# State read and four-expert causal attention on one core: new orders for the five instruction queues

## Chip, cores, metric

One core of one Trainium2 chip. The metric is device time in microseconds (us), the median of repeated runs of one launch; lower is better.

## What is computed

`x` is (8 batches, 8 heads, 512 tokens, 64) and `state` (8, 8, 32, 64). A first attention reads in both directions; its result, 544 rows of 512 for each batch, is the input of a mixture of four causal attention experts, of which every row uses two.

```python
a = softmax(x @ state.T / 8); xread = a @ state        # 512 rows per head
a2 = softmax(state @ x.T / 8); sread = a2 @ x          # 32 rows per head
y = concat([xread, sread])                             # (8, 544, 512)
logits = y @ w_gate; w = softmax over the two largest logits
for e in range(4):
    q, k, v = y @ wq[e], y @ wk[e], y @ wv[e]
    out += w[e] * (softmax(causal(q @ k.T / 8)) @ v @ wo[e])
```

## The kernel before, in words

Most factors are kept as a pair of fp16 numbers, a high part and the rest, and a product of two such pairs is three matmuls (`PROD`, line 293). An op that makes a pair is `split`, `low` or `hi_lo` (lines 338 to 365): one instruction writes the high part, another the difference.

The work on a batch is in four groups.

- `front(b)` (line 556) splits and turns x, makes the scores against the state and their softmax (tiles `eb`, `sbm`, `et`), turns them (`at`), folds the weights into the state (`gs`), and from these makes values `v`, gate logits `lg`, keys `kt` and queries `qm`. `gate` (line 879) is a chain of short instructions over tiles `cmp`, `gt`, `gs`, `wgt`: differences, comparisons, sums, an exponential on ACT, a division.
- The main group: `probs` (line 919) makes scores of a block of 128 rows in PSUM, adds the mask and takes the row maximum on DVE (`masked`, the custom operation in the profile, out `p`), shifts (`mx`), exponentiates on ACT, splits into `ph` and transposes by DMA into `pt`. `reads` (line 963) multiplies by `v`, scales by the gate (`su`, `c`, `z`), splits (`zh`, or `zhp` for two blocks at once), transposes by DMA, and `result` (line 1021) multiplies by `wo` and writes out (`o`).
- `side(b)` (line 846) makes the state's own reads (`a`, DMA to `a2t`, PE into `xt_tail`).
- `tail(g)` (line 1063) does the attention of the 32 state rows of two batches at once (tiles that begin with t).

Nothing in this code fixes the order of the work. Each function records steps (class `Steps`, line 142); a step has an engine, one or more calls and the steps that it must follow. 1883 steps are recorded, and `run` (line 255) then issues them by three packed lists, `ORDER` (line 22): the order of all steps, for each step which of its alternative ways is used, and for each buffer which slot of its tile it gets. A way is another engine for the same operation (`either`, line 208, offers for instance ACT, POOL or DVE for a copy, and DVE or POOL for a difference) or, for a group of matmuls, the reverse order of its two halves. Each engine runs its own steps in the order of the list: 290 steps on PE, 654 on DVE, 527 on ACT, 238 on POOL, 174 DMAs on the SP queue. A step waits for its inputs and for the readers of the buffer that had its slot before.

```python
        for n in memoryview(steps).cast("H"):
            s = self.all[n]
            for f, kw in s["ways"][ways[n]][2]:
                f(**{k: v.ap() if isinstance(v, View) else v for k, v in kw.items()})
```

`takes_port` (line 191) marks steps for the planner that made the lists, and issues nothing: every POOL step, DVE differences and products with both inputs in SBUF, and DVE copies from SBUF to SBUF. Those steps are called port steps below. As all instructions come from line 265 of the loop above, the profile tells them apart by tile names.

Of the kernel before, what the change touches and what calls it, by code (L numbers as in the profile page):

```python
# [24 lines left out]
        "Uq}Y&AUCFlT;K;Gm>ddVN>~jQARB~27FY?ZAQjYt+E53|LmoU06`>LohD=ZjJs<(p1%=9R7D_-yC=F2%4aFe_3Swz2gkjhissKP$H~{tF3@}uK"
        "a}W%%kQWMLVrT;Ap*~!IOHdseKvSpzp;!}&U_-bJA&?)kLoqxAhoLAof_88buE15e2G=1E1VVZ^0>$wLbcPbx0k%U|2*)0f7nRCFN9YMHp*{41"
        "a?l&PKt3#q-Czy0g4VDXx<ednfj*EQ-_k)C05_p8?0^8+3H_iy41~ql3<g0bSc*%qIShs&5Q(>-7=*(zYyr1nISz#txDj?i1g^x2I2y)485{=t"
        "VIK?!qp9FQBVZ(qg2_+{rbAKK26tc&l!R3{1u9`>bQFcrxEklfZnz6$VFBEO888iI!a|q@YcK}KK{8qd;~^m}h7%BriK#4B!8WiJ=E4N1ik>tZ"
        "+QJf;16g4nOoT?b7L(9Ym;~$4mm1@8SOx{*5qQxGSdZ1P2|k7Q@ED%JGuRC8s3~rOlaPo$Ky~~G-c%ct(sO8r51=`|hL`XH%Hb=hgKr=V-a-rf"
        "0daT=KEY?Gk6)lXeuWy?05@PwybljyBPOSx@CzDZ1>A(c;RkKOcvKhT({HMUopBx4!ydR9x8f&ihd$H=dtp~>iGQFy_QVAAhg#uh8i3ufFQ%Zc"  # L30
        "G!Q%BAp8s6@f*B@Id~MN<5cX8-=QD&$H6!RhvG17jsKtzrljFG0!QK~oQxf@4W^<gNH_!M;xwFx{sfqoQd3);iJfp3GS0{G=tm1MK2E>{n1;I2"
        "XiP^l<O>O=r-bN<ir*-J#$aYxh$+#q8+E6Nn1>SKSe%68Fare=VqTh!Ug(WJ*n_^4!=DsHi!eLoqKuS}wqb5cg}>-M?ZoZ419zbZ9)k~*gZ@%#"
        "48oq2pW@+e+=qK{5AMeU=!Y3Gm_AY_I*i95k}^{oEI>Kw2xg&wbPyxqC?>{ZxR$e0T0Dc<s29~IU}fVVIDx^~n~;yA<5)V0(Nu=ka12G!Sv-V&"
        "C<zh^GZ&<!m<dZ$W(=jWw1H1y13HHuT#+krW$sJsIh;;o77U}p6pypwMlMI^F@z$h3UA_u)SUb=K3~MESe*J%A<Bl^cn|O73z!ZYQDZ7eRk;Ku"
        ";39MvxAQ%GgL`=wU&AJJAJgMzzK(HJk;;=VKEUjF32)#4s>V0*EpFjTREnzeJG_N6r2<u^DpZvA@k4x%33(t@r4Lw)a$q$|j)SN=)u5KNl|Nz)"
        "Zbz3fCl02XREug;Gpa*PsRgy74&=$Zxjpr#)|8an&<^fM$+#{(!g@565^+twg2Tv{lk+G1j9#3A1F#kkry(?gQgR)x%_FH3rNG-bibm67@#e=^"
        "m-n*|x1|I8jyuzPKFG&71CF7@e3Zx0SbBm<I2F$oKfZ%y;1D0-!<<%*^LYA#^W+CEkTm?6Pw;%2KojXFPNK=Qh`!<n?m`Rc7cP^NoSJ`Qab8UR"
        "vVi{J5^AJtC>cJ*61<hB&?!F6CHV{o;#yikOKCYRqjj{N((+0Q;Ds`kmdi)pNEvw>ZKn<7&%ykO&+;ZJ!b@Z`?VxnBi_*({$-=8>8hyhIoR!mY"
        "4lV$>`6cG$Je-UFVo}b^`8X5*!}Oe=Gjo81@lGns1-Kv=;$oaZ0y%<LNDLR|5Dw*1yqZe$bUMdN1?Ux?=L<Yb%5gXc$_#pjGbxg1ODxZ#*)&Jy"
        "&?0H9WjKzrad}1x;*}D`7x_8vru7meSNIssrFpcEuJa|n%B$o!t(G;iR<iRRBHAGP=^7uPjB=AN^E!#<%<^8o;~hRhw>Sbi=ndW|C+RL%;Cg(J"  # L40
        "HpyN(L<yvo-sTU|fa`M>X~?Ij5r35C`iwuxX=3t_2D*h>^Jn?OhpC0O*2dg~6Ut`slxF;#w@5sRFJJiuH|6Ghh91%pI!bM|qqgCf{E8n@TYgN{"
        "tOY-zVEH2V_$;;4tCUF|@mBdN5BNSmrN`Wk-|#c)!fo^gc2aLSN7tw&U#D;Kn!oW+{?5PnH$UO_+EQ;&d;Y=O<PSgOr~H?nQwRRX-S{ST<W>xV"
        "LXudviwTQJO1VYJC98PJ4oM^_q$}U1opOm%iH|f<mDG|=l1L|Za)+AgcM*EaIV7ia=UsA{lFASHCCxOu_{mTCEx9C*bmo1MTMo-^>8uUxnB<jw"
        "a-NP$F6_YvC7JZ(zT8z0$qU*q`K2EpkpA37hjKybr9Jg7_2NC^D;KDMbkif!LmS%^p32>|w-%BCJdE#Aj11@FdQ|SyKu#ljr8if#$1;uk=yX1z"
        "u~JSNYFUYs!V)SWQba~@QMn*9cqCVs2GUmt@l1XxeYl~`;@LckYe-F5z~!Zu)wSBzP%29!sUVHzq+XOK(odU8C8=(&<c-vl{(4I5*<fyB6{U&{"
        ";f1`2U(0B2A_MfPEaox%R%+O5d?r_<s$7*~a*-O@bE#=Bq_)(tCHzi`%OxoxC8d;HmOpZZ&Isx?IVWf3pMd@q($c~@LQlwO6&<LmVe*p3vgvg>"
        "t!K2FyrQNSF7@ra4AL=rQk>S2Q&Lx6({1t4I}#yxCB7!m8#0l{@nDUVA$n8l$t3pFTari<>OJWw&Fr+?mqj{M<7rD7spHv8JIMp-EDxovHMcn&"
        "s7radHj^M-#>2FWyrCA>(lTm&S<YQ$E<ciB&7_$%ize4mI*(UqEAiHq+QwQ-N<FIs#7A3MDjlndwY5#q)Vjt}sGl~MHZoDy+BjXR10}64*0xec"
        "2FZ9`q7Nvmp3^kyujw?K4%c<oLMG`vouZR<uq4rT*51<Vd|tupZN5&`1$tg5^9D<*m-K?}(+)O7mT7j)sZp{}12nhh(j$6Mr|B%+X!|vTCex1Q"
        "tDWqSZnAcgNAu}XovwLxwhonH(q1}9e%-By^?)AJ&bCU&$VKg9U2Ts};LWyL%V;+lE8V4s%+VP-PWI|$ov9zSkbc$i@<l)C1c}lD`dPneNiD1^"  # L50
        "d7?~`$r7zSrJ#P-ANo^&X(?T+AsVXdG)C9xDlV$)^|!`q5&ic+(P(5~V#PFCw%8Q;qY3S=4zMdaS4*p>g=t^uX5DRr7S|H$ZQE_IZ8c{ew#|0f"
        "M)k5Bx=GbGYa;6>X2YewjF8oQRR`J-^RaN<qC0h~Zqw}=<aTIpOKO4E!+P2-y{^5atj4oGHpsHL8=A~+>NSmTi7kowT98%MzLwl>YgU)dRnrKK"
        ")LYum?r1r^tG(==X0!y>->U0<O<~zxu=SQ)?tw0|8k*f|YG%viGFfi-P&2yamc!+7QzeJxv|5_e<#qX7epg!;TNcY@S?!TN)+ahm;&h3vu-ul?"
        "QrS{lV5zN-)X@UY&kDLUR=|Q?K`Ue{Ev*%{5c9W@lG%k?5zAwFZMtN$B5su}w5K{s^4V%zWIJuQ?XsfwOb^)}D`v&*h@G|)Hr7hoVJokdG@Xr>"
        "0GHqP+CF=(`|W@owPSYN3c14WyoI=fcGg1O8LOZttg=?ob5_cVx(u$E3v@A7QA^teyJE#%33t*;x>D|jz0lGw%-ykD7Hehgrj@hXcG)i3MGJRV"
        "?XF$32p8$fxH!9S4{f}Cu(}#%6D-ONwNv)MqFszDZ=dY5#kzW0!S2}?8*U%1tQ%%uZKO@K(Kf~=+aw!dQ|ysFws8Ay*X@UmvX?r}BJ7oZv!C|M"
        "Uh5lut5a>7O}7~~(`H#k`)#vrj?J}s_SBx)b1UcSYZ<F#aqgYYw-@$apICYK(jqOrRd5wuC0E&1wpaGoURxFSL94oWF2MfSKLhuFR~)-HR?Ss+"
        "Q5N4Na0#6_Pp8gYBIo6jx*E>gRj~|~%tc#G_ttz}a+kuTbUx0xRL;Y_v-g(RrFQ-<iA(4FTzZ$rrFH)S)?}nA"
    ),
    (  # L60
        "c-obfiw=b#3`05n|Bt?jqI6?$k(j8w)^07dW{vz4IzBW#D^+Z~n{Tr<Adq{ZKUc5fsxqRQPrRQO9O3=$0QNm6r*!~?7_o82KhE&D<AaWR43Ow`"
        "P8cnGx1P+vYJ)`HqeJXdeo8UPxok6*iPBOg+M@#)g&gFFI10F!C>DcTy+Q=a1YaeSR6M3~%lPSx0L#3xt5f6x&Se$}Eescf$;`z3-rj9Ng&0@X"
# [3 lines left out]
        "c-m!?2W|sF3<K5m{~w2=bqWyMNNx*7iq!4QW@ejZTAJBf>oM%#$D_^7)4a#3$8)v3o%Zn3cU$mD2krHzMy&-n{Sj1%NC7QEM54E=M5zdugmC_="
        "ZWc%8W3eLEZcjqWp1vF!wLcQ)fTDqDR4|5(Qei6!Scqp$OBDeY<vf?b_p=VmDz|OjV^1a1=}>~|SS07La{%C4H7!g9eIDuv3VJ+I2b{2Uq~W7H"
        "?_Xm1E}fFn*PyQ8sP0}Y%49;m?Vu!z=K~f*x}!A2pb{d|PII1!+mmzt$U|F|tjkvfsNnLM^)&2{nooyHErxK;XeA~)d?62JhD!?WIbrxaI7M@u"
        "ykZL7Qho;BP%~u6nJL+fLio!~>IdH#sK&8)Qz@#Kv!=z*YEMWmY2m&*#1MGKah7X}vF;51lbEm2i>{!~Gcg-OU;k|vL(~oY&~3uV(D{w3JoL}@"
        "vBN>i%udsYl-w}gt210FBQ+ZIgA0I{YDM&VYgp0l>S;Cj3Owt&v-e89SK)i`?B+JU0A-K{b^"  # L70
# [1153 lines left out]
```

## Time and profile before

| what | value |
|---|---|
| median of 3 runs (least to most) | 282.70 us (282.16 to 283.89) |
| the profiled execution's own time | 282.6 us |
| span of the profile, first to last instruction | 280.8 us |
| granted TensorE clock, mean over the span | 1.000 |
| busy: PE, DVE, ACT, POOL | 266.9, 253.0, 227.3, 180.6 us |
| chain that ended last, by engine | PE 58%, DVE 16%, ACT 10%, DMA 7%, POOL 5% |

A timeline row gives start and duration in us, engine, line, operation, the tile written and the tiles read, shapes, how many instructions were merged, and in brackets how long the engine stood idle before and what ended that. A group row gives the count, the busy time in us, the mean in ns, and the idle time before. A row of the chain gives start, length and what was on the path.

### The profile page before, as it was taken

How to read it: one execution, taken by the hardware profiler on the slowest of the kernel's cores; microseconds unless marked ns; L12 is line 12 of the kernel's file. 1: busy time of each engine (PE TensorE's matmuls, PEld its weight loads, DVE VectorE, ACT ScalarE, POOL GpSimd, SP SyncE). 2: the span in 40 equal slices, each digit the busy share in tenths (PEclk: the TensorE clock that was granted, in tenths of full speed). 3: DMA queues.
4: the chain of work that ended last, by engine and by line, in shares of the span. 5: the costliest groups of instructions: out<-in, count | busy, mean ns of one | idle time of the engine just before them, and what ended most of it. 6: DMA issues, size and time to landing. Idle time of an engine off the chain costs nothing.

```text
span 280.8 us, 9174 instructions
## 1 busy us (share of the span) xinstructions
PE 266.9 (95%) x3441; PEld 177.4 (63%) x3441; DVE 253.0 (90%) x748; ACT 227.3 (81%) x627; POOL 180.6 (64%) x251
## 2 busy tenths in 40 slices
...
GB/s 199 241 153 150 166 172 190 237 191 153 157 200 191 188 168 248 172 197 171 207 235 260 131 239 161 167 173 118 205 236 154 154 245 193 225 219 189 213 226 157
DMA packets 163853, 53.70 MB, mean 191 GB/s; under 512 B 142688, under 2 KB 159328, under 8 KB 163808
## 3 DMA queue, kind: packets, MB, share of 16 engines
...
## 4 chain that ended last, share of the span: by engine, by line
PE 58%; DVE 16%; ACT 10%; DMA 7%; POOL 5%; issue 3%; SPq 0%; DVEq 0%; POOLq 0%; ACTq 0%
PE bank L265 58%; DMA a2t<-a 4%; DVE xh L265 2%; DMA pt<-ph 2%; ACT p L265 2%; DVE eb L265 1%; DVE sbm L265 1%; DMA xn<-in_x_dram 1%; POOL ph L265 1%; POOL eb L265 1%; DVE a L265 1%; ACT v L265 1%; DVE et L265 1%; ACT kt L265 1%; POOL at L265 1%
## 5 line engine op out<-in xcount | busy, mean ns | idle before, releaser
L265 ACT ACTIVATE p<-p,mx 128x256 f32<-128x256 f32 (+3 forms) x88 | 45.9, 557 | 3.1 <-POOL mx L265 2.3
L265 PE MATMUL bank<-gs,at 128*128 128x260 f16 (+3 forms) x296 | 40.7, 285 | 1.7 <-DVE z L265 1.6
L265 PE MATMUL bank<-v,pt 128*128 128x65 f16 (+1 forms) x660 | 40.8, 218 | 0.9 <-DMA pt<-ph 0.5
L265 PE MATMUL bank<-kt,qm 64*128 64x128 f16 (+7 forms) x384 | 40.5, 298 | 0.8 <-DVE z L265 0.6
L265 PEld LDWEIGHTS <-pt 128*128 128x128 f16 x660 | 37.7, 98 | 5.7 <-issue 2.3
L265 POOL TENSOR_TENSOR ph<-p,ph 128x1024 f16<-128x1024 f32 (+1 forms) x19 | 38.4, 2021 | 3.8 <-ACT tlg L265 1.3
L265 DVE CUSTOM_DVE_ANT_0 p<-bank,band 128x384 f32<-128x384 f32 (+3 forms) x88 | 39.4, 480 | 1.0 <-PE bank L265 0.6
L265 PE MATMUL bank<-at,gs 128*128 128x512 f16 (+1 forms) x128 | 32.7, 393 | 0.5 <-DVE v L265 0.5
L265 PEld LDWEIGHTS <-qm 64*128 64x128 f16 (+1 forms) x384 | 19.8, 95 | 18.0 <-issue 8.0
L265 PEld LDWEIGHTS <-at 128*128 128x128 f16 x264 | 25.1, 97 | 9.2 <-issue 2.1
L265 PE MATMUL bank<-wo_n,z 128*128 128x512 f16 (+1 forms) x114 | 26.1, 368 | 1.1 <-DMA z<-zh 0.5
L265 DVE SCALAR_TENSOR_TENSOR xh<-xn,xh 128x512 f16<-128x512 f32 x28 | 21.3, 778 | 1.5 <-ACT xh L265 0.9
L265 PE MATMUL bank<-wo_n,zp 128*128 128x512 f16 x84 | 20.1, 380 | 0.0
L265 ACT ACTIVATE ph<-p 128x1024 f16<-128x1024 f32 (+1 forms) x20 | 19.7, 983 | 0.2
L265 PEld LDWEIGHTS <-gs 128*128 128x128 f16 x120 | 11.4, 98 | 12.2 <-issue 1.2
L265 ACT ACTIVATE o<-bank 128x512 f32<-128x512 f32 (+1 forms) x30 | 16.9, 575 | 1.8 <-PE bank L265 1.2
L265 PEld LDWEIGHTS <-z 128*128 128x128 f16 x114 | 10.6, 98 | 12.0 <-issue 1.9
L265 POOL TENSOR_TENSOR at<-et,at 128x512 f16<-128x512 f32 x10 | 12.7, 1274 | 6.0 <-DVE cmp L265 4.2
L265 PEld LDWEIGHTS <-xh 128*128 128x128 f16 x416 | 14.1, 98 | 3.9 <-DVE xh L265 1.4
L265 ACT ACTIVATE v<-bank 128x256 f16<-128x256 f32 x40 | 15.4, 403 | 1.3 <-PE bank L265 0.8
L265 ACT ACTIVATE gs<-bank 128x260 f16<-128x260 f32 (+3 forms) x33 | 15.7, 491 | 0.6 <-PE bank L265 0.5
L265 ACT ACTIVATE z<-bank,c 128x64 f32<-128x64 f32 x62 | 13.9, 331 | 2.6 <-POOL c L265 1.6
...
## 6 DMA issues: line engine op xcount, KB each, us to landing
...
pt<-ph SPq DMA_TRANSPOSE x30, 4.1
...
```

The source lines that it names most:

```text
L265: f(**{k: v.ap() if isinstance(v, View) else v for k, v in kw.items()})
```

## The change

Only the three packed lists differ; configuration, steps and calls are the same. Cut to its form:

```diff
@@ -21,53 +21,53 @@
 ORDER = (
     (
-        "c-jru1A7o^7y!`M-@@7!mR75^wQO#=p`n&-+qP}nwr$(CZM%Da#d(f5!~=r(V1OXt18E>3tOb9_3ArH&6ag<t3l4HXK1c)^pb)Hs^{@dvAt|H)"
...
+        "c-jTQ17HwP6ac{IzZO=l<ytkgS}j|PtF^7Rw3cn#wr$(CZQHhO+$9D8hIo(z3_PGPB!PSo9~9C-0$2;a-~|r+AQ7a8gpdr%LLiiaVvrI_f;VJ?"
...
```

Unpacked and set against the old lists (a step counts when the step before it on its engine is another one): 33 of 290 steps on PE follow another, 141 on DVE, 109 on ACT, 84 on POOL, 43 on the SP queue. Of the ways, 50 differ: 23 steps come to DVE and 16 leave it, 15 come to ACT and 18 leave it, 9 come to POOL and 13 leave it, and three groups of matmuls have their halves reversed. Of 962 buffers, 576 get another slot, 300 of them PSUM banks. From 98 to 180 us and after 228 us the order on PE is the old one. The differences that the prediction speaks of (step number, what it does, its start in the profile before):

```
start, 0 to 60 us
  eleven of the twelve warm-up matmuls (line 514) PE: changed places among themselves
  109, 380, 370  single matmuls, 36.31, 54.35, 54.46
                                                  PE: up to eight places earlier
  13   copy of the state tile sn, 6.32            ACT -> DVE, second there
  118  copy of v out of a bank, 22.48             ACT -> DVE
  122  copy of lg out of a bank, 23.65            ACT -> DVE
60 to 98 us
  766  DMA xT<-xh, 67.40                          SP: six places earlier
  768  maximum m<-bank, 774 turn eb<-bank, 72.12 and 73.36
                                                  DVE: from ahead of 636 to behind it
  636  difference a (then DMA a2t, PE step 638)   DVE: as above
  571, 589  PE values and a small product, 77.97  PE: from ahead of 638 to behind step 478 (83.69)
  616  PE product, 80.57                          PE: to behind 278 (86.20)
  643  PE xt_tail,wn, 89.20                       PE: from ahead of 618 (92.37) to ahead of 493 (84.69)
  593  sum gt<-cmp, 495 reciprocal su, 88.42 and 88.34
                                                  DVE: 593 now ahead of 495; 597 still next
  597  gt<-gt,gt, 88.74                           DVE, same neighbourhood
  475, 468  z sum and ph difference, 88.26, 88.70 POOL, still one behind the other
  578  v difference, 87.35, and 949, 955          DVE: 578 to behind 497 (91.75); 949 ahead, 955 behind
180 to 228 us
  1484 DMA a2t<-a, 176.22                         SP: four places earlier
  934  z sum, 187.96; 1486 a difference (two instructions), 193.38; 924 zh difference, 166.75
                                                  POOL: all three directly behind 1485 (180.33)
  925  DMA z<-zh, 186.11                          SP: ahead of 1289 (184.36)
  1226 copy of lg, 182.21                         ACT -> DVE
  1241 cmp, 184.66                                DVE: three places earlier
  1294 masked p, 185.73                           DVE: from ahead of 1247 to behind it
  1247 gt<-gt,gt, 186.42                          DVE, still behind 1292
  1130 PE v,pt, 188.46                            PE: from ahead of 1316 (188.97) to behind 926 (190.34)
  1128 ph difference, 195.21                      DVE -> POOL
  1709 sum s, 196.30                              ACT -> DVE, directly behind 1304 (195.00)
  1711 a, 199.63; 1330 mx, 206.45; 1144 zhp, 209.77
                                                  POOL -> ACT
  1715 a difference (two instructions), 206.23    DVE -> POOL
  1352, 1345  PE v,pt, 211.08 and 214.14          PE: each one or two places later
  1158, 1159, 1160 z and zh, 207.10, 207.64, 222.57
                                                  POOL: ahead of 1301 (202.84)
```

## Rows read from the trace of the kernel before

**Rows 1.** Busy time by engine in four stretches: us, then each engine, clock, DMA.

```profile
25.00:60.00 35.00, 34.32 (x514) 23.57 (x499) 33.53 (x91) 33.37 (x91) 24.34 (x37) 1.00 0.90 189
60.00:98.00 38.00, 34.65 (x481) 24.00 (x480) 36.34 (x99) 32.55 (x99) 27.02 (x33) 1.00 1.02 179
98.00:180.00 82.00, 81.99 (x1005) 54.96 (x1003) 78.68 (x236) 69.89 (x202) 60.81 (x72) 1.00 1.05 195
180.00:228.00 48.00, 45.62 (x653) 28.88 (x652) 45.19 (x144) 41.31 (x112) 35.48 (x41) 1.00 0.87 179
```

**Rows 2.** Chain that ended last, 21 to 36 us: start, us, what.

```profile
22.58 0.28 ACT v L265
...
24.77 10.00 PE bank L265 x221
```

**Rows 3.** Timeline, 88 to 93.3 us: start, us, engine, line, operation, tiles.

```profile
88.26 0.48 POOL L265 TENSOR_TENSOR z<-z 128x128 f32<-128x128 f32 x1 [3.42 <-ACT su L265]
...
88.42 0.22 DVE L265 TENSOR_REDUCE gt<-cmp 128x20 f32<-128x80 f32 x1
88.70 2.13 POOL L265 TENSOR_TENSOR ph<-p,ph 128x1024 f16<-128x1024 f32 x1
88.74 2.13 DVE L265 SCALAR_TENSOR_TENSOR gt<-gt,gt 128x20 f32<-128x20 f32 x1
...
92.37 1.16 PE L265 MATMUL bank<-gs,at 128*128 128x256 f16 x9 [1.60 <-DVE z L265]
```

**Rows 4.** Tile gt: one group of its instructions, ns least/median/most.

```profile
L265 DVE SCALAR_TENSOR_TENSOR gt<-gt,gt x9: 115/171/2129, 27.0 to 264.3; 128x16 f32<-128x16 f32 x5, 128x20 f32<-128x20 f32 x3, 128x4 f32<-128x4 f32 x1
```

**Rows 5.** Timeline of DVE, 184 to 189 us.

```profile
186.42 1.61 DVE L265 SCALAR_TENSOR_TENSOR gt<-gt,gt 128x16 f32<-128x16 f32 x1
```

**Rows 6.** Timeline of PE, 186 to 194 us.

```profile
190.34 1.47 PE L265 MATMUL bank<-wo_n,z 128*128 128x512 f16 x6 [0.48 <-DMA z<-zh]
192.38 0.83 PE L265 MATMUL bank<-kt,qm 64*128 64x384 f16 x12 [0.57 <-DVE z L265]
```

**Rows 7.** Timeline of POOL, 167.5 to 171 us.

```profile
167.82 0.69 POOL L265 TENSOR_SCALAR a<-e,s 128x512 f16<-128x512 f32 x1
168.47 1.05 POOL L265 TENSOR_SCALAR xn<-xn 128x512 f32<-128x512 f32 x1
```

**Rows 8.** Timeline of DVE, 167.5 to 171 us.

```profile
168.06 0.98 DVE L265 SCALAR_TENSOR_TENSOR xh<-xn,xh 128x512 f16<-128x512 f32 x1
```

**Rows 9.** Chain that ended last, 198 to 232 us.

```profile
222.63 4.93 DMA pt<-ph
...
227.61 4.61 PE bank L265 x51
```

**Rows 10.** Chain that ended last, 66 to 82 us.

```profile
72.21 0.60 DVE m L265
72.81 1.22 DVE eb L265 x2
...
74.96 4.16 DMA a2t<-a
```

**Rows 11.** Timeline of PE, 92 to 100 us.

```profile
97.67 1.46 PE L265 MATMUL bank<-wo_n,z 128*128 128x512 f16 x6 [0.39 <-DVE gs L265]
```

**Rows 12.** Timeline of POOL, 178 to 193 us.

```profile
180.33 0.69 POOL L265 TENSOR_SCALAR a<-e,s 128x512 f16<-128x512 f32 x1 [2.08 <-DMA a2t<-a]
185.23 1.16 POOL L265 TENSOR_TENSOR at<-et,at 128x512 f16<-128x512 f32 x1 [4.21 <-DVE cmp L265]
186.35 1.64 POOL L265 TENSOR_TENSOR ph<-p,ph 128x768 f16<-128x768 f32 x1
```

**Rows 13.** Timeline of POOL, 199 to 228 us.

```profile
199.63 0.69 POOL L265 TENSOR_SCALAR a<-e,s 128x512 f16<-128x512 f32 x1 [1.91 <-DMA a2t<-a]
...
206.45 0.57 POOL L265 TENSOR_SCALAR mx<-mx 128x2 f32<-128x2 f32 x1
...
209.77 1.26 POOL L265 TENSOR_SCALAR zhp<-z 128x256 f16<-128x256 f32 x1
```

**Rows 14.** Groups by line and form, POOL: count, busy us, mean ns, idle before.

```profile
L265 POOL TENSOR_TENSOR ph<-p,ph 128x1024 f16<-128x1024 f32 x11 | 24.6, 2238 | 1.5 <-ACT tlg L265 1.3
```

**Rows 15.** Groups by line and form, DVE.

```profile
L265 DVE TENSOR_TENSOR ph<-p,ph 128x1024 f16<-128x1024 f32 x9 | 11.2, 1242 | 0.5 <-ACT ph L265 0.3 <-POOL ph L265 0.2
L265 DVE SCALAR_TENSOR_TENSOR a<-e,s,a 128x512 f16<-128x512 f32 x14 | 10.7, 762 | 1.5 <-POOL a L265 1.2 <-ACT a L265 0.2
```

More of the change, by code (lines that the diff above doesn't have):

```diff
@@ L23 @@
     (
-        "c-jru1A7o^7y!`M-@@7!mR75^wQO#=p`n&-+qP}nwr$(CZM%Da#d(f5!~=r(V1OXt18E>3tOb9_3ArH&6ag<t3l4HXK1c)^pb)Hs^{@dvAt|H)"
[L25 to L58, printed above, removed]
-    ),
@@ L60 @@
-    (
-        "c-obfiw=b#3`05n|Bt?jqI6?$k(j8w)^07dW{vz4IzBW#D^+Z~n{Tr<Adq{ZKUc5fsxqRQPrRQO9O3=$0QNm6r*!~?7_o82KhE&D<AaWR43Ow`"
-        "P8cnGx1P+vYJ)`HqeJXdeo8UPxok6*iPBOg+M@#)g&gFFI10F!C>DcTy+Q=a1YaeSR6M3~%lPSx0L#3xt5f6x&Se$}Eescf$;`z3-rj9Ng&0@X"
-        "#_$~v6*;@QN`xw-stl*X?#$LIQ}f!96pc^bS{trnRTVPWg8z9WpRdnRjOqXKAba>GQ%>lz6PMdfe&eV*PBj*5AMD$;H!dc^0rmrh5CJ&"
-    ),
-    (
[L66 to L70, printed above, removed]
+        "c-jTQ17HwP6ac{IzZO=l<ytkgS}j|PtF^7Rw3cn#wr$(CZQHhO+$9D8hIo(z3_PGPB!PSo9~9C-0$2;a-~|r+AQ7a8gpdr%LLiiaVvrI_f;VJ?"
@@ new lines @@
+        "To?k$p&;ah;*bV1KyJ(mVNe=MKyL5{A6N(LVFP4@w2%q{paMigYAB2;pcWK@%8(yd!YWt|wc#{`Lkv^_f&%CX2z5Z96xM~aP!Ov^X)J@)pgL59"
+        "%uo-`Kpv<8=b%0ufLJ&W5zrW#LQN=yLC^$>;00&^m*654#fESh4nrJVfva#0isKO|h9&S2G=g?;9Xi7e=m6WHEVhSG>;Xxk7v#Z`*cG~fQeNx`"
+        "Eg=|oz)r{oMPUs@LKJj@T~G;nLo4V8MIaM|!dvPNTOc3ygx#<h4?-Up0DYk!^oN146q~^k90Y@52;77)Yz=#%95#nrFcjLrGW4JpFdA;dax}UF"
+        "D=-Gj<9^r(ZDANx!F@0lhQkOL38P>#ti<WC4OZb4sDSff4~zjvCtwClgPBkj??O1P#s#njXTd!f3*%rRjE9OCfz_}&`p_bX#JP}w64GLr0P|or"
+        "OoXH~3GzZCTmoxx4io@yT8GK$9j(X4SOb^BGVr2JkchUza(Dzy@F_foC-4kbz<X$hC*c9a;&a#x$*49q#n<o>KEOI|jvMeJB&HYe3Zk$Kyn(k+"
@@ new lines @@
+        "2T#Ed_ynJ!K7N4|bRSw^5~_p`p(a+wckmM$U>t75Ul5NPVqN?SKPVb&;TGJ4p7fhKV-M_t^{^do#;q8i{?Kpeg<bI*e4;<l65C@>{7kLzD-FQD"
+        "*a441Z|sKOVIU5|l=K(6V{7b)b8tHL!>QN?`{Q67f<y5iWQSqc2MLE`DjI<!aWam=DL5AaQ_~EbhVyWSq@lJr6Md-@GNz|lI3LGjTJpqnlz{}}"
+        "V@4W{iVH9SPQY)J3cHeFH=2ll=?mp1#7r~>6JmFojgv4D`cW3>K?`v#jzcfZPX6?h@=yRJ#+>w>Qe$4qMGieMkhbAY+>Sf&80^CLlm<Ug2<4-A"
+        "m;`s@K3s%paWC${{dfQaFc9-oX8K4$bQq6A4ho|qn1y~(I?PH(@gMah<p>I<UUU#MV^TbW$M6KE$82;QPhxLEHV&uy1YDlHaSb~r7CwZ`$uJ1d"
+        "VgV{mS+D`ca39*hW$6^2!z$d6Dv}3R<@H>F3Q;`Hihb!kmZNGMj2qb(xA7jniX~_#U%*D>$z`Z8oyKcekT&sMypG#>Gw<blcmo?#Hr&D&u^(l?"
@@ new lines @@
+        "wOpOEV@WDPO(>G?V<=t1{1Bgu(ja<+QB;WrPz+V32Uvsm@lD*tx3CKJr&xZA(NvX+(K}3z)#yDY;DPiIt5XfSj2|!sHm6b)OEoD3>(WQefrF_f"
+        "ZRI$sMYX98HKV3fkA_k^Do!ov5hmmgG*jBs5b8*+s5K?yMC`*UxF#p($JmCvIF5I7M%=-}C=;gSPxu*Y@o-ATbvQA1qPo1FM^J4ZNuwwU`{8YT"
+        "#|L;c9po`|jF0j-8cRv}IH%?-I9J-zc>00!<O`<dL;Ri>%MqSW>G&shrZoHu5A#P}AdBb;eqe82Na^JcPN2m!k;=m)noM6YCHl$&I>BA&H!hPu"
+        "c#=zSBR$1SXbo+pZy3rY*#}SaQ#`{fXelkHW%QY+&{|5*>nIbir-ibTe0d{fkc<+@%VisFr%zmz&+-OZBAIy;?VzmekGp6yO{HnHiu^d3LpTHH"
+        ";vAftbMkz7iGQ&e=i$5@#Q!iO=i@A#Ny_j}isbxUfD3YQ_7i_D$19{F7vjQPgiG;iD$UdB94{51S9qQ;@GObqvg|K2=o!wWFrF<DJd0-29GOFl"
```

31 lines of the change are left out of this document (added).

## The prediction, made before the changed kernel ran

> **What bounds the kernel now.** I read the busy times by stretch first [rows 1]. From 98 to 180 us PE has 81.99 us of work in 82.00, so nothing that happens on other engines there can show. It stands idle for 35.00 − 34.32 = 0.68 us between 25 and 60, for 38.00 − 34.65 = 3.35 between 60 and 98, and for 48.00 − 45.62 = 2.38 between 180 and 228. The new lists leave PE its work, so apart from the start these 6.4 us are the ceiling of any gain. In both idle stretches DVE is the busiest of the others (36.34 of 38.00, 45.19 of 48.00): it sets when PE can go on. At the start the chain of waits goes through copies on ACT, one of them a `v` of 0.28, until PE takes over at 24.77 for 10.00 us [rows 2].
>
> Then I looked for what ends PE's idle time. The longest is 1.60 us before the product at 92.37, ended by DVE's `z`. Up the DVE queue from there stands one instruction on 20 columns that took 2.13 us, from 88.74 to 90.87 [rows 3]. Its group has a median of 171 ns [rows 4], so 1.96 us of it were a wait inside the instruction. POOL had begun a subtraction 0.04 us earlier, at 88.70, and ended it at 90.83 [rows 3]. The same happens at 186.42: 1.61 us, 1.44 of them lost [rows 5]; PE then idles 0.48 at 190.34 and 0.57 at 192.38 [rows 6]. A DVE step with two inputs in SBUF that comes just after a POOL step stands until that ends.
>
> Who goes first when DVE already waits? POOL ran `a` from 167.82 to 168.51, the next POOL instruction is shown from 168.47 with 1.05 us [rows 7]; DVE's difference `xh` came at 168.06 and ended at 169.04 [rows 8]. DVE waited for the first and went ahead of the second. So the loser of a collision is whoever arrives after the other's start, and a waiting DVE step passes one POOL step, not two.
>
> Last, PE's 50 us of unbroken work to the end start at 227.61, behind a DMA `pt` of 4.93 us that POOL released at 222.6 [rows 9]. A gain made before that must also reach POOL there.
>
> **The change, part by part.** Sums are against the profiled execution, 282.6 us (span 280.8 and 1.8 around it); the median of the runs is 282.7.
>
> *Start.* Steps 118 and 122 leave ACT, and with 118 the 0.28 that stood on the chain [rows 2]: −0.3. The state copy 13 moves too, but PE's next step then waits for the input DMA anyway; nothing. The warm-up matmuls and the single matmuls 109, 380 and 370 change places beside waits of other engines; nothing. Bounds: −0.68, PE's whole idle time up to 60 [rows 1], and +0.3, if the copies come as late on DVE.
>
> *60 to 98 us, ahead of 638.* DVE made 768 (0.60) and 774 (half of 1.22) before 636, and 636 releases the DMA `a2t` of 4.16 us for which PE stands at 79.16 [rows 10]. With both behind it the DMA starts up to 1.21 earlier, or somewhat less, since 636 also needs ACT's high part. But 571 and 589, about 1.1 us of PE work, no longer fill that wait: PE loses up to 0.5 there. They are not lost: with 616 and 643 they now stand behind 638, where PE later waited. DMA 766 is earlier, but what follows it on PE waits for an ACT copy: nothing.
>
> *The step 597.* The sum 593 is put ahead of the reciprocal 495. 597 needs 593, which came last before it (88.42 to 88.64) [rows 3]. The reciprocal needs a copy from ACT that ends only as POOL starts the `z` sum, step 475. So in the new order 597 is ready about 0.2 us sooner in relation to POOL, while 475 (0.48 us) still runs, and passes 468. I take it that it does: DVE gains up to 1.96, PE loses its waits of 1.60 [rows 3] and 0.39 at 97.67 [rows 11]. With the 0.5 above: −1.5. If 597 arrives after POOL's start, all is as before and the 0.5 remains: +0.5. Best case −3.35 [rows 1]. The margin is some 0.2 us; I take −1.5 as the later PE steps also stand behind the freed DVE.
>
> *180 to 228 us.* POOL stood idle 2.08 us before 180.33, for a DMA, and 4.21 before 185.23 [rows 12]. DMA 1484 is issued earlier, which ends the first wait sooner, and 934, 1486 and 924 are put into the second, at a time when DVE works mostly from PSUM. 925 then has its data some 2 us before the old issue at 186.11: PE's 0.48 goes. 1226 and 1241 start the gate chain earlier, and 1294 (0.55) is moved behind 1247. So 1247 arrives while POOL still does the `at` difference that ended at 186.39, not just after the `ph` difference began at 186.35 [rows 12], and it passes the latter: 1.44 us less on DVE, and the 0.57 goes. Together −1.05 [rows 6]; 1130, moved behind 926, fills what is left. Bounds: −2.38 [rows 1], and +0.6, about one POOL step of `at` size (1.16) by half, if the filled POOL is late with `at`.
>
> *POOL up to the DMA `pt`.* POOL loses 0.69, 0.57 and 1.26 (1711, 1330, 1144) [rows 13] and gains 1715, which as two instructions costs 0.69 + 1.16 by like steps [rows 12]: −0.67. 1160 comes from behind to the front and 1143 into an idle time, about even. I count it as 0, and it has to carry a gain of up to 0.67 by itself; the rest by starting earlier.
>
> *Moves from DVE to POOL.* 1128 takes 2.24 on POOL [rows 14] and 1.24 on DVE; 1715 1.85 against 0.76 [rows 15]. Each frees DVE but puts a long port step beside it. An ordinary hit costs about 0.98 − 0.76 = 0.22, the difference of 0.98 [rows 8] against a like form's mean [rows 15]; a hit by a step twice as long may cost more, so I take 0.3 for each, +0.6 for two on the path; bounds 0 and +2.1, below. The other moved ways are of 0.1 to 0.6 us beside free time, or lie between 98 and 180; nothing.
>
> The Trainium skill (SBUF — State Buffer, section "Who interferes with whom") says that issue order alone decides who blocks, and for the whole instruction. The trace agrees on the two long collisions (2.13 and 1.61), and says more than the page: a waiting DVE step passes a queued POOL step (169.04). By the page alone POOL might keep its turn, and the time would be that of rival 1.
>
> Sum: −0.3 − 1.5 − 1.05 + 0 + 0.6 = −2.25, from 282.6 to 280.35, or 280.4 by the median.
>
> **Rivals.**
> 1. *Both collisions stay*: 597 and 1247 still meet POOL's step just begun. For it: 0.04 us decided before, and 475 and 468 moved with their neighbours. Against it: both were re-placed on the side that helps. −0.3 + 0.5 − 0.48 = −0.3: 282.3.
> 2. *The wait moves to the DMA `pt`*: PE comes earlier to 227.6 and waits there, since POOL has little slack before 222.6. Then only POOL's 0.67 is gained: 281.9. Against it: part of POOL's work itself waits for PE and DVE, and moves with them.
> 3. *Most idle time goes*: two thirds of 3.35 + 2.38, and the 0.3: −4.1, 278.5. Against it: many waits end within 0.1 us of each other, so behind one gone stands the next.
> 4. *Slower: POOL's new long steps hold DVE.* At 195 us 1128 runs 2.24 on POOL, and the first step behind 1304 on DVE is now 1709, a short port step (a like one has 0.17 [rows 4]); behind it in DVE's queue are the maximum `mb`, the `c` and `z` products and evictions for which PE waits. If 1709 arrives after 1128 has begun, DVE stands up to 2.1, less the 1.24 that it was freed of: +0.9. The same at 1715: 1.85 − 0.76 = +1.1. With collisions as before and nothing else: 282.6 − 0.3 + 0.9 + 1.1 = 284.3. It decides from the point where the stand of DVE is longer than the work it was freed of. The Trainium skill (Perfetto Trace Analysis, section "Optimizing Scalar/DVE Operations") says that moving work between these two engines might not help, as they share a port; the rows on collisions agree.
>
> **How the numbers follow.** Forecast 0.40 (280.4; its own range 279.3 to 281.6), rival 1 0.17, rival 2 0.13, rival 3 0.18, rival 4 0.12. About 1% is what a measurement of this kernel tells from no change: faster is below 279.9, slower above 285.5. Faster: rival 3 and a third of the forecast, 0.31, say 0.32; slower: the upper part of rival 4 and what I have not seen, 0.08; same 0.60. The range goes from rival 3 to a little above rival 4's price, 278.3 to 284.4.
>
> **What would show it.** In the profile after, the two `gt<-gt,gt` instructions of batches 2 and 6 near their old places take 0.2 us, not 1.6 and more; PE's idle time in its products near 90 us ended by DVE `z` is gone; the `z<-zh` wait near 190 is gone; PE enters its last unbroken stretch near 225.4. Wrong it is if one of the two stays long, if PE waits more than 1 us for `pt` at the last stretch, or if a small DVE step near 195 or 205 takes over 1 us.

## The result, and the profile after

The median is 279.37 us against 283.29 of before (20 runs each). The ratio is 0.9877 with a 95% interval of 0.9855 to 0.9899: 3.5 us faster, by the interval 2.9 to 4.1. The ratio compares the means, 279.67 against 283.14 us, without the two slowest runs of the changed kernel (282.95 and 283.96); the medians lie 3.9 us apart. The profiled execution took 278.83 us with a span of 277.0, where that of before took 282.6 with 280.8; the difference of the two traces that has to be found is 3.8.

The same four stretches of the kernel after, columns as in [rows 1]:

```profile
25.00:60.00 35.00, 34.45 (x492) 23.68 (x477) 34.33 (x93) 33.71 (x90) 23.18 (x32) 1.00 0.94 199
60.00:98.00 38.00, 34.39 (x485) 23.39 (x490) 36.29 (x100) 33.39 (x98) 29.98 (x32) 1.00 0.91 168
98.00:180.00 82.00, 81.86 (x1006) 55.23 (x1003) 79.06 (x239) 69.34 (x197) 60.80 (x71) 1.00 1.10 201
180.00:228.00 48.00, 47.56 (x684) 30.24 (x684) 46.20 (x155) 44.14 (x120) 36.86 (x40) 1.00 0.91 196
```

Between 180 and 228 us PE's idle time fell from 2.38 to 48.00 − 47.56 = 0.44. Between 60 and 98 it did not fall at all: 38.00 − 34.39 = 3.61, where 3.35 stood before. Measured between two products that are the same in both kernels, those at 60.03 and 97.67 before, the stage took 37.64 us before and 37.30 after (59.22 to 96.52). The stage for which I had forecast the largest gain gave 0.3 us, and the other gave more than all I had forecast for it.

PE's timeline of the kernel after says where the idle time now stands:

```profile
64.03 1.76 PE L265 MATMUL bank<-kt,qm 128*128 128x128 f16 x24 [1.37 <-DMA qm<-qh]
...
90.35 1.45 PE L265 MATMUL bank<-wo_n,z 128*128 128x512 f16 x6 [1.70 <-DVE xt_tail L265]
...
96.52 1.46 PE L265 MATMUL bank<-wo_n,z 128*128 128x512 f16 x6 [0.24 <-DVE gs L265]
...
187.98 1.46 PE L265 MATMUL bank<-wo_n,z 128*128 128x512 f16 x6
...
189.88 0.83 PE L265 MATMUL bank<-kt,qm 64*128 64x384 f16 x12
```

The product at 96.52 is the one of 97.67 [rows 11]: 1.15 us earlier. The two at 187.98 and 189.88 are those of 190.34 and 192.38 [rows 6]: their waits of 0.48 and 0.57 are gone, and the second is 2.50 earlier. Ahead of 98 us stand two waits that are together about as long as those removed there: 1.37 for a DMA `qm`, and 1.70 for DVE's `xt_tail`.

The chain that ended last, in the kernel after:

```profile
211.34 1.30 ACT p L265 x3
...
212.72 1.05 POOL ph L265
...
216.44 2.11 POOL ph L265
...
218.58 5.06 DMA pt<-ph
...
223.68 50.25 PE bank L265 x620
```

The same piece of the chain before, up to the DMA `pt`:

```profile
214.37 0.34 DVE p L265
...
215.41 1.30 ACT p L265 x3
...
216.78 1.04 POOL ph L265
```

The DMA `pt` is still the last link ahead of PE's unbroken work, as in [rows 9], but POOL releases it at 218.58, not 222.63, and PE enters at 223.68 where it entered at 227.61: 3.93 us earlier.

Now the two collisions. DVE's timeline of the kernel after, at both places:

```profile
87.53 0.18 DVE L265 SCALAR_TENSOR_TENSOR gt<-gt,gt 128x20 f32<-128x20 f32 x1
87.63 2.10 DVE L265 TENSOR_TENSOR c<-su,wgt 128x6 f32<-128x6 f32 x1
...
90.00 0.29 DVE L265 SCALAR_TENSOR_TENSOR xt_tail<-bank,xt_tail 64x128 f16<-64x128 f32 x1
...
184.56 0.17 DVE L265 SCALAR_TENSOR_TENSOR gt<-gt,gt 128x16 f32<-128x16 f32 x1
```

and POOL's:

```profile
87.57 2.14 POOL L265 TENSOR_TENSOR ph<-p,ph 128x1024 f16<-128x1024 f32 x1
...
183.53 1.16 POOL L265 TENSOR_TENSOR at<-et,at 128x512 f16<-128x512 f32 x1 [3.64 <-ACT at L265]
184.65 1.66 POOL L265 TENSOR_TENSOR ph<-p,ph 128x768 f16<-128x768 f32 x1
```

At 184.56 step 1247 comes while POOL still runs `at` and takes 0.17, as forecast. At 87.53 step 597 comes 0.04 us ahead of POOL's difference and takes 0.18, not 2.13 [rows 3]: also as forecast. But 0.10 behind it comes the product `c` (step 496), the next port step of DVE, on 6 columns. It begins 0.06 after POOL and stands 2.10. `xt_tail`, behind it in the queue, frees the bank for which PE waits 1.70. In this profile the collision was not removed, it was passed on by one instruction.

### The profile page after: what moved, and what is told of

Same layout as the page of the kernel before. It is cut to its first block, busy times and chain, and to the rows that moved or that the text cites. A ratio compares the mean times of both kernels' runs of the same rounds, so it can differ in the third digit from the quotient of the medians.

```text
span 277.0 us, 9171 instructions
## 1 busy us (share of the span) xinstructions
PE 266.0 (96%) x3441; PEld 178.0 (64%) x3441; DVE 251.3 (91%) x755; ACT 227.7 (82%) x619; POOL 184.3 (67%) x250
## 4 chain that ended last, share of the span: by engine, by line
PE 62%; DVE 21%; ACT 7%; DMA 4%; issue 2%; POOL 2%; DVEq 0%; POOLq 0%
PE bank L265 62%; DMA qm<-qh 2%; DVE mb L265 2%; DVE m L265 2%; DMA pt<-ph 2%; DVE gs L265 2%; DVE eb L265 2%; DVE qf L265 2%; DVE xh L265 1%; DVE a L265 1%; DVE p L265 1%; POOL ph L265 1%; DVE sbm L265 1%; POOL at L265 1%; DVE v L265 1%
## 5 line engine op out<-in xcount | busy, mean ns | idle before, releaser
L265 ACT ACTIVATE p<-p,mx 128x512 f32<-128x512 f32 (+3 forms) x88 | 45.4, 555 | 1.9 <-POOL mx L265 1.7
L265 POOL TENSOR_TENSOR ph<-p,ph 128x1024 f16<-128x1024 f32 (+1 forms) x20 | 40.2, 2009 | 4.4 <-ACT ph L265 2.8
L265 PE MATMUL bank<-v,pt 128*128 128x65 f16 (+1 forms) x660 | 41.4, 218 | 0.6 <-DVE mx L265 0.4
L265 DVE CUSTOM_DVE_ANT_0 p<-bank,band 128x256 f32<-128x256 f32 (+3 forms) x88 | 39.4, 480 | 1.1 <-PE bank L265 0.5
L265 ACT ACTIVATE ph<-p 128x1024 f16<-128x1024 f32 (+1 forms) x21 | 20.5, 977 | 0.7 <-DMA pt<-ph 0.5
L265 DVE SCALAR_TENSOR_TENSOR xh<-xn,xh 128x512 f16<-128x512 f32 x27 | 19.0, 720 | 0.0
L265 ACT ACTIVATE o<-bank 128x512 f32<-128x512 f32 (+1 forms) x28 | 16.1, 579 | 1.5 <-PE bank L265 1.2
L265 ACT ACTIVATE v<-bank 128x256 f16<-128x256 f32 x39 | 14.6, 391 | 2.8 <-PE bank L265 2.7
L265 ACT ACTIVATE gs<-bank 128x512 f16<-128x512 f32 (+3 forms) x32 | 15.4, 500 | 0.3 <-PE bank L265 0.2
L265 ACT ACTIVATE z<-bank,c 128x64 f32<-128x64 f32 x56 | 12.6, 328 | 3.1 <-POOL c L265 2.9
```

## Experiments

Theory after the two traces: 1.2 us of PE's lead are won ahead of 98 us and 2.7 behind 180, and the two add; in the stage of 60 to 98 us a POOL difference of 2.1 us makes one DVE port step stand, whichever it is. Rivals: the late gain is a consequence of the early lead; or one of the two collisions carries it all. The order lists are packed, so each edit is shown as what it does to the queue of its engine.

**New lists in front, or behind.** Two kernels splice the two sets of lists near 140 us, where both have the same order on PE; buffers that live across the splice keep their slots.

```diff
e1_new_first:  steps ahead of 140 us
- old order, ways, slots
+ new order, ways, slots
e2_new_second: steps behind 141 us
- old order, ways, slots
+ new order, ways, slots
```

> The new lists up to about 140 us (orders, ways and slots), the old ones behind. Theory, from the two traces: PE's lead grows to 0.8 us by 60, by 0.35 more from 60 to 98, by nothing to 180, and by 2.7 from 180 to 228, and these parts don't depend on each other. Then this kernel is 1.2 us faster than before (0.9 to 1.5; ratio about 0.996), its lead at 180 is about 1.2, and the collision at 186.4 (about 1.6 us for one gt step) is there or not by chance. Rival: the late gain is a consequence of the early one (everything arrives sooner and misses the collision); then most of the 3.9 us is gained here.

> The old lists up to about 141 us, the new ones behind. Theory: the late stage gives its 2.7 us alone (2.2 to 3.0; ratio about 0.991), PE enters its last unbroken stretch near 225.0, the gt step of batch 6 near 186 takes 0.2 us. Rival: without the early lead the late steps come in another relation to POOL and less than 1.5 us is left.

Measured: e1 has a ratio of 1.0009 (0.9985 to 1.0032), no gain where the theory had 1.2 us; e2, as the theory had it, 0.9904 (0.9873 to 0.9935), median 279.85 against 282.61, 2.8 us. Busy time by engine from 180 to 228 us, e1:

```profile
180.00:228.00 48.00, 45.19 (x650) 28.53 (x648) 45.29 (x144) 41.31 (x113) 35.75 (x41) 1.00 0.82 177
```

and e2:

```profile
180.00:228.00 48.00, 47.50 (x693) 30.58 (x686) 46.32 (x153) 44.02 (x121) 36.92 (x40) 1.00 0.92 197
```

e2 has the idle time of the changed kernel there (0.50), e1 that of before or more (2.81). The late gain needs no early lead: in e2 PE even came to the product of 97.67 at 98.07. And e1 shows what an early lead is worth alone. PE came to that product at 96.80, 0.87 earlier, and then, in PE's timeline of e1:

```profile
190.30 1.47 PE L265 MATMUL bank<-wo_n,z 128*128 128x512 f16 x6 [0.88 <-DMA z<-zh]
...
227.60 0.91 PE L265 MATMUL bank<-v,pt 128*128 128x65 f16 x24 [0.98 <-DMA pt<-ph]
```

It waited longer for the same two transfers, and entered the last stretch at 227.60, where the kernel before enters at 227.61. That is the mechanism of rival 2, with the old lists behind. The interval leaves room for a gain of 0.4 us, so the early part of the theory failed and the late part held.

**Batch 2: who stands at POOL's difference.** Three single edits.

```diff
e3_sum_first (kernel before), DVE:
  856 a
- 495 reciprocal su
  593 sum gt<-cmp
+ 495 reciprocal su
  597 gt<-gt,gt
  496 c
e4_ph_later (changed kernel), POOL:
  475 z sum
+ 483 z sum
  468 ph difference
  615 m
- 483 z sum
e6_xh_later (changed kernel), DVE:
  481 c
- 955 xh difference
  595, 640, 856, 593, 495, 597, 496
+ 955 xh difference
  780
```

> The kernel before with one edit: on DVE the sum 593 goes ahead of the reciprocal 495. Theory A (the collision is passed on): step 597 takes about 0.2 us instead of 2.13, but the product 496 right behind it is the next port step, arrives after POOL's difference 468 has begun, and takes about 2 us; time within 0.3 us of before. Rival B (the forecast): DVE is free, PE's 1.60 us before 618 goes, 1.2 to 1.9 us faster. Rival C: 597 is still caught (2.1 us), time as before.

> The changed kernel with one edit: on POOL the z sum 483 goes ahead of the ph difference 468 (which then starts about 1.4 us later; its transfer is not issued until 3.6 us after its end in the changed kernel). Theory: the product 496 on DVE takes 0.15 us instead of 2.10, PE's 1.70 us before the product at 90.35 goes, and the kernel is 0.8 to 1.4 us faster than the changed one. Rival: the short steps of the gate (601 to 604) come just after 468 has begun and are caught for up to 2 us; gain under 0.5 us.

> The changed kernel with one edit: on DVE the difference 955 (0.68 us; its transfer is not issued until 89.08) goes from ahead of 595 to behind 496. Then 597 and 496 come some 0.4 us before POOL's 468 can begin. Theory: 496 takes under 0.4 us instead of 2.10, PE's 1.70 us goes, 0.8 to 1.6 us faster than the changed kernel (ratio to before about 0.983). Rival: the collision is only passed on once more, to 955 (over 2 us) or to the gate's 601 (over 1 us); gain under 0.5 us.

e3: ratio 1.0029 (1.0002 to 1.0057), no gain. Theory A's mechanism held; the time is 0.8 us longer than before, where it had said within 0.3, and the cause of that stays open. DVE's timeline of e3 (POOL's `ph` difference began at 89.35):

```profile
89.33 0.18 DVE L265 SCALAR_TENSOR_TENSOR gt<-gt,gt 128x20 f32<-128x20 f32 x1
89.42 2.11 DVE L265 TENSOR_TENSOR c<-su,wgt 128x6 f32<-128x6 f32 x1
```

e4: 0.9961 (0.9933 to 0.9989), median 281.16: slower than the changed kernel (0.9877), not faster: the theory missed. `c` took 0.16 and PE's 1.70 went, but POOL's difference began at 89.03, and later a second POOL step at 92.25. DVE's timeline of e4:

```profile
87.65 0.16 DVE L265 TENSOR_TENSOR c<-su,wgt 128x6 f32<-128x6 f32 x1
...
89.64 1.56 DVE L265 TENSOR_TENSOR wgt<-gt,gs 128x20 f32<-128x20 f32 x1
...
92.52 1.70 DVE L265 TENSOR_SCALAR m<-twg 128x4 f16<-128x4 f32 x1
```

The rival was right about the gate's 601 (1.56), and nobody had named 646 (1.70), which in the changed kernel passes with 0.18 us to spare. PE then waited 2.35 us for a `v` behind them, and its clock fell (last section).

e6: 0.9899 (0.9863 to 0.9935), median 279.32: the changed kernel's time. DVE's timeline of e6 (POOL's difference began at 87.28):

```profile
87.28 0.15 DVE L265 TENSOR_TENSOR c<-su,wgt 128x6 f32<-128x6 f32 x1
87.35 2.62 DVE L265 SCALAR_TENSOR_TENSOR xh<-xn,xh 128x512 f16<-128x512 f32 x1
...
93.59 1.77 DVE L265 TENSOR_SCALAR m<-twg 128x4 f16<-128x4 f32 x1
```

Passed on once more, to the step that I had moved out of the way: the rival's case. 646 stood as well (1.77), behind a POOL step that began at 93.43, and PE waited 1.92 and 1.42 us. But the profiled execution took 281.39 us; four of e6's six runs took 279.02 to 279.33, and what stood in those no profile shows.

So in each of the eleven profiles in which 468 is in its place on POOL, exactly one DVE step stands about 2.1 us or more at it: 597 in two (before and e2), 955 in one (e6), 496 in the eight others. Three of these eight run the old lists in this stretch (e7, e8 and e11, below): there 597 passed without any edit, as it began 0.06 to 0.07 us ahead of POOL's difference and not 0.04 behind it. In the kernel before, too, it was a toss-up of some 0.1 us which of the two stood, and the stand was as long.

The stage as a whole did not cost the same, though. From the product of 60.03 to that of 97.67 it took 37.57 to 37.64 us in before, e2 and e3, and 36.64 to 36.79 in e7, e8 and e11; all six have the old lists there, but for e3's one edit. A second toss-up lies earlier in the stage. Timelines of DVE and POOL, before:

```profile
82.65 2.72 DVE L265 SCALAR_TENSOR_TENSOR xh<-xn,xh 128x512 f16<-128x512 f32 x3
83.70 1.14 POOL L265 TENSOR_SCALAR ph<-p 128x1024 f16<-128x1024 f32 x1 [1.15 <-ACT p L265]
```

and e7:

```profile
83.60 1.88 DVE L265 SCALAR_TENSOR_TENSOR xh<-xn,xh 128x512 f16<-128x512 f32 x3
84.86 1.53 POOL L265 TENSOR_SCALAR ph<-p 128x1024 f16<-128x1024 f32 x1 [1.35 <-ACT p L265]
```

DVE's three `xh` take 2.72 also in e2 and e3, and 1.88 also in e8 and e11. The 0.84 us fits the difference of the stage; no edit tested it. In the changed kernel POOL's `ph` takes 1.63 there and DVE does not stand, yet the stage takes 37.22 to 37.31 in the four profiles with the new lists unedited up to there (changed, e9, e1, e12). So the new lists are not better in this stage than the old ones were when that toss-up fell out well.

**The same difference on DVE.** The direct way to be rid of the collision is to have no 2.1 us POOL step there.

```diff
e5_ph_dve, e10_ph_dve_again (changed kernel):
 POOL
- 468 ph difference
 DVE
  646 m<-twg
+ 468 ph difference
  574 v
e9_after_again: the changed kernel, no edit
```

> The changed kernel with POOL's ph difference 468 given to DVE, behind step 646 there. Theory (the 60 to 98 us gain was eaten because POOL's 2.1 us difference holds whichever port step of DVE comes next): with no long POOL step there 597, 496 and 601 all take under 0.3 us, DVE pays 1.24 and saves 2.0, PE's 1.70 us before the product at 90.35 goes; 0.5 to 1.2 us faster than the changed kernel (ratio to before about 0.985). Rival: the 1.24 us delays the copies 574 and 578 for which PE's next bank waits; PE stands there over 1 us, and the time is that of the changed kernel or worse.

> The changed kernel with POOL's ph difference 468 on DVE, again, for a profile. Theory: no port step of the gate between 86 and 92 us takes over 0.4 us, PE's 1.70 us is gone, 0.5 to 1.1 us faster than the changed kernel. Rival: another wait of PE of over 1 us stands between 88 and 97, and the time is the changed kernel's within 0.3 us.

> The changed kernel once more, for a second profile beside the two kernels derived from it. Theory (which port step stands is decided by some 0.05 us at 87.6 and some 0.2 us at 93.2, so it can fall out differently from run to run): most times near 279.3, a few 2 us or more above; in the profile either 597 or 496 of batch 2 takes about 2 us, and the late stage looks as in the first profile (PE idle under 0.6 us from 180 to 228). Rival: the late gain itself comes and goes.

e5's profiled execution took 926.43 us and says nothing of the others; its ratio is 0.9876 (0.9833 to 0.9919). e10 has 0.9892 (0.9852 to 0.9931) and a median of 279.02; e9, measured beside it, 0.9892 (0.9860 to 0.9923) and 279.54, with two of its six runs at 281.17 and 281.35, as its theory had a few. In e9's profile 597 took 0.18 and 496 took 2.09, and PE was busy for 47.40 of the 48.00 us: the late gain is there again. In e10's profile none of 597, 496 and 601 takes over 0.2 us. DVE's timeline of e10:

```profile
91.60 1.21 DVE L265 TENSOR_TENSOR ph<-p,ph 128x1024 f16<-128x1024 f32 x1
```

and PE's:

```profile
93.20 0.84 PE L265 MATMUL bank<-wn,bd 64*32 64x512 f16 x23 [0.64 <-DVE v L265]
```

PE's 1.70 has gone and 0.64 has come, as the rival had it, though it had said over 1. PE comes to the product of 97.67 at 95.98, 0.62 before e9; but this is the shortest of e10's seven runs (278.19). By the medians 0.5 us may be gained, by the intervals nothing is shown. A version that beats the changed kernel was not found.

**180 to 195 us: the two edits of the forecast.**

```diff
e7_mask_later (kernel before), DVE:
  1243 gt<-cmp
- 1294 masked p
  1292 masked p
  1247 gt<-gt,gt
+ 1294 masked p
e8_mask_and_dma: the same, and SP:
+ 925  DMA z<-zh
  1289 DMA pt<-ph
- 925  DMA z<-zh
```

> The kernel before with one edit: on DVE the masked maximum 1294 (0.55 us) goes from ahead of 1292 to behind 1247. Theory: 1247 comes about 0.5 us sooner, while POOL still runs the at difference that ends at 186.39, stands until that ends at most and passes the ph difference 1119: it takes under 0.7 us instead of 1.61, PE's 0.57 us before the product at 192.38 shrinks, 0.4 to 1.2 us faster than before. If the whole late gain of 2.8 us hangs on this collision, 2 us or more faster. Rival: PE's wait for the transfer before 190.34 stays and takes the gain; within 0.3 us of before.

> The edit of the run before plus one on the SP queue: the transfer 925 goes ahead of 1289. Theory (the forecast's sum of the two): PE's 0.48 and 0.57 us both go, 1.0 to 1.3 us faster than before; the remaining 1.6 us of the late gain come from edits behind 195 us. Rival: the whole 2.8 us.

e7: 0.9988 (0.9961 to 1.0016), the rival's result. The long stand is gone: in DVE's timeline of e7 1247 came 0.45 before `at` ended on POOL (185.39 + 1.16), stood until then and passed the `ph` difference.

```profile
186.10 0.48 DVE L265 SCALAR_TENSOR_TENSOR gt<-gt,gt 128x16 f32<-128x16 f32 x1
```

But PE then waited for the transfer instead. PE's timeline of e7:

```profile
190.97 1.47 PE L265 MATMUL bank<-wo_n,z 128*128 128x512 f16 x6 [0.87 <-DMA z<-zh]
```

e8: 0.9968 (0.9947 to 0.9989), 0.9 us. PE's timeline of e8 shows neither wait:

```profile
189.37 1.46 PE L265 MATMUL bank<-wo_n,z 128*128 128x512 f16 x6
190.84 0.99 PE L265 MATMUL bank<-kt,qm 64*128 64x384 f16 x12
```

From the product of 97.67 to this `kt,qm` e8 took 190.84 − 97.27 = 93.57 us, the kernel before 94.71, the changed one 93.36. The two edits together make nearly the whole of this step's gain; the first alone makes 94.54. The second alone was not run.

**Behind 195 us.**

```diff
e11_late_only: steps behind 191 us
- old order, ways, slots
+ new order, ways, slots
e12_two_back (changed kernel):
 POOL
- 1128 ph difference
- 1715 a difference
 DVE
  1304 masked p
+ 1128 ph difference
  1709 sum s
...
  1650 sum sbm
  1440, 1490
+ 1715 a difference
  1473 kt
```

> The old lists up to about 191 us, the new ones behind (1128 and 1715 on POOL, 1709 on DVE, 1711, 1330 and 1144 on ACT, 1158 to 1160 earlier on POOL). Theory: the late gain has two parts that add, 1.2 us up to 195 and 1.6 us behind; here the second alone: 1.2 to 1.7 us faster than before, PE's waits of 0.52, 0.28 and 0.53 us (201.56, 213.39, 227.61) gone, those at 190.34 and 192.38 there. Rival: behind 195 the gain needs the earlier one; under 0.6 us.

> The changed kernel with the differences 1128 and 1715 on DVE again, behind 1304 and behind 1650, as in the kernel before. The forecast had them on POOL cost 0.6 us and its slower rival 2.0: by these this kernel is 0.6 to 2 us faster than the changed one. Theory after the two traces: on POOL they cost next to nothing (no DVE step beside them stands over 0.4 us), and DVE, freed of 1.24 and 0.76 us, is what removes PE's waits at 201.56 and 213.39: this kernel is 0.5 to 1.2 us slower than the changed one.

e12: median 280.69 against e9's 279.54, measured beside it: 1.15 us slower than the changed kernel. By the ratios (0.9923, 0.9896 to 0.9951, against 0.9892, 0.9860 to 0.9923) it is 0.9 us, and the intervals overlap a little; the forecast's 0.6 us to the other side is outside e12's. So the direction is as the theory after the traces had it. The waits are not: those of 201.56 and 213.39 did not come back. DVE reached the masked `p` that it begins at 209.20 in the kernel after at 212.27, 1.15 us more than the 1.92 by which e12 was already behind at the turn of `eb` ahead of the edit (190.38 and 192.30), POOL came as much later to the DMA `pt`, and in e12's timeline PE waited there:

```profile
227.10 0.91 PE L265 MATMUL bank<-v,pt 128*128 128x65 f16 x24 [0.43 <-DMA pt<-ph]
```

Why the long POOL step costs nothing is in DVE's timeline of the kernel after, while 1128 ran on POOL from 190.63 to 192.77:

```profile
191.05 0.27 DVE L265 CUSTOM_DVE_ANT_0 p<-bank,band 128x128 f32<-128x128 f32 x1
...
192.21 0.28 DVE L265 CUSTOM_DVE_ANT_0 p<-bank,band 128x128 f32<-128x128 f32 x1
...
192.42 0.37 DVE L265 TENSOR_SCALAR s<-s 128x2 f32<-128x2 f32 x1
```

Four masked maxima read PSUM and take beside it what they take in e12 with POOL idle (0.27, 0.55, 0.55 and 0.28). The port step 1709, rival 4's victim, comes when 0.35 us of POOL's 2.14 are left, and takes 0.37. Beside 1715 (203.02 to 204.96) DVE's steps take what they take in e12, where 1715 is not on POOL.

e11 was a miss: 1.0113 (1.0088 to 1.0139), 3 us slower than before. PE's timeline of e11:

```profile
195.76 2.41 PE L265 MATMUL bank<-v,pt 128*128 128x194 f16 x18 [2.48 <-ACT e L265]
```

and ACT's:

```profile
194.93 0.69 ACT L265 ACTIVATE e<-bank,m 128x512 f32<-128x512 f32 x1 [2.32 <-POOL a L265]
```

The new lists put this exponential early in ACT's queue, and its tile is free only when POOL's second `a` difference (1486) has read it. In the changed kernel 1486 stands in POOL's idle time and ends at 179.27; in e11, with the old lists there, at 194.90. So the late lists can't do without that early move, and e11 says nothing of what they give alone.

Starts of three products in all profiles but e5's: `wo_n,z` (97.67 before), `kt,qm` (192.38) and the first `at,gs` of the last stretch (230.44):

| kernel | first at | to the second | to the third |
|---|---|---|---|
| before | 97.67 | 94.71 | 38.06 |
| changed | 96.52 | 93.36 | 36.60 |
| e9, changed again | 96.60 | 93.43 | 37.02 |
| e1 | 96.80 | 95.14 | 38.46 |
| e2 | 98.07 | 93.21 | 36.66 |
| e3 | 98.26 | 94.75 | 38.53 |
| e4 | 98.60 | 93.37 | 37.11 |
| e6 | 98.53 | 93.37 | 37.38 |
| e7 | 97.83 | 94.54 | 37.48 |
| e8 | 97.27 | 93.57 | 38.10 |
| e10 | 95.98 | 93.37 | 36.71 |
| e11 | 97.26 | 94.71 | 41.22 |
| e12 | 98.41 | 93.39 | 38.11 |

The second column is 93.2 to 93.6 where both early edits are in, and 94.5 to 95.1 where one or both are missing. The third is 36.6 to 37.4 with the two POOL moves, and 37.5 to 38.5 without, e11 aside; e12, which lacks these two moves alone, has 38.11, as much as the kernels that lack all late edits. The first column scatters by 1.9 us among kernels with the new lists unedited up to there (96.52 to 98.41), and by 0.8 with the old, so one profile can't resolve a gain in it; the 98.41 is e12's, whose profiled execution took 282.10 us, the longest of its six.

## Why the forecast was right in direction and wrong in two of its terms

I forecast −2.25 us by the trace; the profiles differ by 3.8 and the runs by 3.5 (2.9 to 4.1). The direction and the range held. The time, 279.37, lies just inside the likeliest case's own range, but as a difference that range ends at −3.3, and −3.5 is nearer to rival 3's −4.1. That is partly luck, for two terms failed in opposite directions. The signs that I named came: both `gt<-gt,gt` short, PE's wait for DVE `z` near 90 and the `z<-zh` wait gone, the last stretch entered early (223.68; I had said 225.4); and none of the signs of being wrong came. They could not catch the stage that failed, as they looked at the two victims and not at what stands in their place.

- *Start, −0.3.* A product at 60.03 before starts at 59.22 after, −0.81. That is past the −0.68 that I had called its bound; but the row that I took it from begins at 25 us and counts nothing before that. With the new lists in front the product starts at 59.19 to 59.62 in six profiles and at 61.10 in e12, with the old at 60.03 to 61.18, so a lead is likely, and its cause was not tried. It does not show in the time: by e1 no early lead reached the end with the old lists behind; with the new ones behind, e2's median is 0.3 to 0.5 us above the changed kernel's (279.54 and 279.37), within the intervals.
- *60 to 98 us, −1.5.* This step failed. "I take it that it does; DVE gains up to 1.96" was right in its first half (597 passed, as it did in e7, e8 and e11 with the old lists) and wrong in the second: I followed one victim and did not ask which port step comes next in the queue. 496 stood, 2.10. Where the price of rival 1 let both collisions stay, here the edit worked and the loss stayed. The 0.5 that I charged for 571 and 589 did not come either: PE's timeline shows no wait between 74.38 and 90.35. (Nor had PE stood long at 79.16 before: the product ahead of it ends at 79.08.) The wait of 1.37 for `qm` I had not seen; its DMA took 5.53 us, was issued 0.80 us earlier than before and took 3.9 there. It takes 5.4 to 5.6 in all seven profiles with the new lists in front and 3.8 to 3.9 in all six with the old. The new lists put the transfer 766 ahead of it on the SP queue, which I had priced at nothing, looking only at what follows 766 on PE. Two transfers of 766's kind take the queue 3.31 us to issue from 52.24, some 1.6 each, which fits the 1.6 us; no run puts 766 back alone, so this cause is not shown.
- *180 to 228 us, −1.05.* Right: 94.71 − 93.36 = 1.35 by the table, of which e8's two edits make 1.14. But I had added 0.48 and 0.57 as if each edit gave its own; by e7 the collision's edit alone gives 0.17 by the table and nothing that could be measured in the time, and what the transfer's edit gives alone was not run.
- *POOL up to the DMA `pt`, 0.* Right in effect: the DMA starts 4.05 earlier, by all of the gain, though POOL's queue had lost only 0.67 of work. What had looked like little slack was POOL waiting for ACT, and ACT for DVE. By the two chains POOL's last run of steps ahead of the DMA takes 5.85 us before (216.78 to 222.63) and 5.86 after (212.72 to 218.58), and begins 4.06 earlier. Rival 2 holds only with the old lists (e1).
- *Moves from DVE to POOL, +0.6.* This step failed too. The sign was wrong; e12 puts the term near −1 (−0.9 by the ratios, −1.15 by the medians). I priced the stand of DVE by an ordinary hit and set it against nothing, though the freed 1.24 and 0.76 us of DVE stood in rows of my own. In a stage where DVE sets when PE can go on they were the larger part. (The upper bound, given as +2.1, is 0.9 + 1.1 = 2.0.) Rival 4's mechanism needs a port step right behind POOL's start; there stood four steps that read PSUM.

The Trainium skill (Perfetto Trace Analysis, section "Optimizing Scalar/DVE Operations") says that offloading between DVE and GpSimd might not help; e12 is a case in which it helped, by about 1 us, with DVE at work from PSUM meanwhile. The Trainium skill (SBUF — State Buffer, section "Who interferes with whom") leaves a DVE instruction with at most one SBUF input out of the contention, unless it runs in a two-port mode; the four maxima agree. 1709 and 646 have one SBUF input as well and did stand (0.37 us where e12 has 0.16; 1.77 in e6), so here the count of inputs alone does not tell who is safe.

With the measured sizes the sum is: up to the first product −1.15 (this profile), then −1.35, then −1.46, and 0.2 lost behind: −3.8. The idle time that rival 3 wanted gone is gone behind 180 us by 1.94 of 2.38, and not at all ahead of 98.
